# A fused RWKV-7 recurrence and MLP: chunks of 64 steps and 64x64 blocks on the quarters of the TensorE array

## The chip, the cores and the metric

The kernel runs on one NeuronCore of a Trainium2 chip, in one launch. The metric is the device time of that launch in microseconds (us), as a median over several runs. All arithmetic is float32. "Clock" is the mean clock that the throttle granted to TensorE, as a share of full speed; "half clock" is time at which it granted 0.5. In this program TensorE does the matrix products (PE in the profiles; PEld are its weight loads), and its results land in tiles of the memory called PSUM. VectorE (DVE), ScalarE (ACT) and GpSimd (POOL) copy and work on them, and SyncE (SP) issues the DMAs.

## The reference

Two blocks follow each other. The first is a recurrence over 768 steps for 4 batch entries and 8 heads of 40 channels. The second is an MLP over the 4 x 768 = 3072 tokens that come out of it.

```python
# r, k, v, w, a, b: (batch 4, heads 8, steps 768, channels 40)
for t in range(S):
    y[:, :, t] = einsum('bhd,bhde->bhe', r_t, state)
    Sa = einsum('bhde,bhe->bhd', state, a_t)
    state = state * w_t[:, :, None, :] - einsum('bhd,bhe->bhde', Sa, b_t) \
            + einsum('bhd,bhe->bhde', v_t, k_t)
x = y.transpose(0, 2, 1, 3).reshape(3072, 320)
h = x @ w_in                                  # w_in:  320 x 2048, given as float64
g = h * (1.0 / (1.0 + np.exp(-1.702 * h)))
out = g @ w_out                               # w_out: 2048 x 320, given as float64
```

## The kernel before

A chunk of C steps is computed at once. With F the product of the decays from the middle of the chunk, the kernel needs scaled inputs (kh, bh, ah), triangular C x C matrices A, N, RV and M for each head, the solution of a triangular system, and a state Z that goes from chunk to chunk:

```
A = tril(ah kh^T, -1),  N = tril(ah bh^T, -1),  SA = (I - N)^-1 (A v + ah Z^T)
(I - N)^-1 = (I + N)(I + N^2)(I + N^4) ...        (one "level" a factor)
Z' = Z + v^T kh + SA^T bh,   y = F (r Z + tril(r v^T) kh + tril(r SA^T) bh)
```

Before, a chunk has 128 steps, and a *unit* is one chunk of one batch entry with its 8 heads; there are 24 units. Heads come in pairs on the 128 partitions. The solve has seven levels.

```python
C = 128; LEVELS = C.bit_length() - 1                        # 7
ps_misc  = tile_pool(name="ps_misc",  bufs=3, space=PSUM)   # single banks of PSUM
ps_solve = tile_pool(name="ps_solve", bufs=3, space=PSUM)
ps_mlp   = tile_pool(name="ps_mlp",   bufs=2, space=PSUM)

def score(dst, lhsT, rhs, low=False):         # A, N, NT, RV, M: 64 rows, 128 columns of the array
    ps = [quad(psum(ps_misc)) for _ in range(2)]
    for q in range(NP):
        for e in range(2):
            p = slice(e * DP, (e + 1) * DP)
            mm(ps[e][:, q, :], lhsT[p, q, :], rhs[p, q, :], q == 0)
    ...                                       # masks
def level(n, e):                              # 128 x 128 products
    NT, N = s["NT"][e], s["N"][e]
    for q in range(NP):
        mm(dx[:, q], NT[:, q], xs[e][:, q], q == 0)          # 40 columns
    ...
        mm(ps[:, q], N[:, q], NT[:, q], q == 0)              # N^2, and the same for NT
# MLP of two finished units: 16 steps of `up`, 8 of `down`
for kt, (o, n) in enumerate(KT):              # 320 channels = 128 + 128 + 64
    nc.tensor.matmul(ph, w_in_sb[:n, kt, f*128:(f+1)*128], xTs[j][:n, kt, :], ...)
for f in range(part * NF // 4, (part + 1) * NF // 4):
    nc.tensor.matmul(po[u], gTs[j][f][:, u*C:(u+1)*C], w_out_sb[:, f, :], ...)
```

The main loop gives each engine its instructions in a fixed order. `weave(main, side)` issues the steps of unit i's solve and spreads two things through them: the preparation of unit i+1, and MLP steps of finished units (or, in the first units, the conversion of the float64 weights). The loads of unit i+2 are issued after the last step of unit i.

```python
for i, (c, b) in enumerate(units):
    ...
    weave(solve(i), mixed(side, mlp))
    load(i + 2)
```

Of the kernel before, what the change touches and what calls it, by code (L numbers as in the profile page):

```python
# [1 line left out]

# [19 lines left out]

# The recurrence, for one head and a chunk of C = 128 steps, with F_t the product of the decays
# from the middle of the chunk up to t (exclusive; its inverse before the middle), per key channel:
#
#   S_t = Z_t diag(F_t),  kh = k / F_{t+1},  bh = -b / F_{t+1},  ah = a F_t
#   A = tril(ah kh^T, -1),  N = tril(ah bh^T, -1)
#   SA = (I - N)^-1 (A v + ah Z_0^T)
#   Z_C = Z_0 + v^T kh + SA^T bh
#   y  = F (r Z_0 + tril(r v^T, -1) kh + tril(r SA^T, -1) bh)  # L30
#
# The decays are positive, so F is the exponential of a sum of logarithms, which a product with a
# constant triangle takes; the middle as its origin keeps F and 1 / F small over the chunk.
# N is nilpotent, so (I - N)^-1 = (I + N)(I + N^2)(I + N^4) ... (I + N^64) exactly.
# Two heads share the 128 partitions of a channel-major tile, 64 apiece, the rest zeros.


def weave(main, side):
    """Issue main in order, with side spread evenly through it."""
    done = 0  # L40
    for i, f in enumerate(main):
        f()
        upto = len(side) * (i + 1) // len(main)
        while done < upto:
            side[done]()
            done += 1
# [3 lines left out]
def rwkv7_gelu_quick(ctx: ExitStack, tc: tile.TileContext, rT_d, k_d, v_d, w_d, a_d, b_d, w_in, w_out, out):  # L50
    nc = tc.nc
    B, S, H, D = k_d.shape
    DM = H * D
    C = 128
    MID = C // 2
    NCH = S // C
    NP = H // 2
    DP = 64
    DFF = w_in.shape[1]
    NF = DFF // 128  # L60
    KT = [(o, min(128, DM - o)) for o in range(0, DM, 128)]
    NK = len(KT)
    PIECE = max(256, DM)
    LEVELS = C.bit_length() - 1
    assert S % C == 0 and H % 2 == 0 and B % 2 == 0 and D <= DP and DFF % 128 == 0 and DM <= 512

# [3 lines left out]
    ps_misc = ctx.enter_context(tc.tile_pool(name="ps_misc", bufs=3, space=bass.MemoryType.PSUM))  # L70
    ps_solve = ctx.enter_context(tc.tile_pool(name="ps_solve", bufs=3, space=bass.MemoryType.PSUM))
    ps_mlp = ctx.enter_context(tc.tile_pool(name="ps_mlp", bufs=2, space=bass.MemoryType.PSUM))
# [4 lines left out]
    def psum(pool):  # L77
        return pool.tile([128, 512], FP32, tag="bank", name="bank")

    quad = lambda t: t.rearrange("p (q t) -> p q t", q=NP)  # L80
    heads = lambda t: t[:, :DM].rearrange("p (h d) -> p h d", h=H)
    halfheads = lambda t: t[:, :NP * D].rearrange("p (q d) -> p q d", q=NP)

    def mm(o, lhsT, rhs, start):
        nc.tensor.matmul(o, lhsT, rhs, start=start, stop=True, skip_group_check=True)  # L85

# [1 line left out]
    ident = single("ident", [128, 128])  # L88
    make_identity(nc, ident)
    upper = single("upper", [128, 128])  # L90
    nc.gpsimd.memset(upper, 1.0)
    nc.gpsimd.affine_select(out=upper, in_=upper, compare_op=ALU.is_gt, fill=0.0, base=0,
                            pattern=[[1, 128]], channel_multiplier=-1)
    lower = single("lower", [128, 128])
    nc.gpsimd.memset(lower, 1.0)
    nc.gpsimd.affine_select(out=lower, in_=lower, compare_op=ALU.is_gt, fill=0.0, base=0,
                            pattern=[[-1, 128]], channel_multiplier=1)
    # [u, t]: 1 where u <= t, less 1 where u is before the middle
    cums = single("cums", [128, 128])
    nc.gpsimd.memset(cums, 1.0)  # L100
    nc.gpsimd.affine_select(out=cums, in_=cums, compare_op=ALU.is_ge, fill=0.0, base=0,
                            pattern=[[1, 128]], channel_multiplier=-1)
    nc.vector.tensor_scalar_add(cums[:MID], cums[:MID], -1.0)
    halves = single("halves", [128, 2])
    nc.vector.memset(halves[:, 0:1], 1.0)
    nc.vector.memset(halves[:, 1:2], 0.0)
    nc.vector.memset(halves[MID:, 0:1], 0.0)
    nc.vector.memset(halves[MID:, 1:2], 1.0)

    upper4 = upper.unsqueeze(1).to_broadcast([128, NP, 128])  # L110
    lower4 = lower.unsqueeze(1).to_broadcast([128, NP, 128])

# [1 line left out]
    nat = [single(f"nat{i}", [128, 4, H, DP]) for i in range(2)]  # L114
    rT = [single(f"rT{i}", [128, NP, 128]) for i in range(3)]
    sn = [single(f"sn{i}", [128, H, DP]) for i in range(2)]
    z0 = [single(f"z0{i}", [128, NP, 2, DP]) for i in range(2)]
    wch = [[single(f"wch{b}{i}", [128, 2, NP, 2]) for i in range(2)] for b in range(B)]
    wz = [single(f"wz{b}", [128, NP, 2]) for b in range(B)]
    zraw = [single(f"zraw{b}", [128, NP, 2, D]) for b in range(B)]  # L120
    for t in rT:
        nc.vector.memset(t, 0.0)
    for b in range(B):
        for t in wch[b]:
            nc.vector.memset(t, 0.0)
    for t in nat:
        nc.gpsimd.memset(t[:, :, :, D:], 0.0)
    for t in sn:
        nc.gpsimd.memset(t[:, :, D:], 0.0)
    for t in z0:  # L130
        nc.gpsimd.memset(t[:, :, :, D:], 0.0)

    w_in_sb = single("w_in_sb", [128, NK, DFF])
    w_out_sb = single("w_out_sb", [128, NF, DM])

# [1 line left out]
    def load_weight(dst, src):  # L137
        P, n = dst.shape
        raw = work.tile([128, PIECE], INT64, tag="raw", name="raw")
        nc.sync.dma_start(raw[:P, :n], src)  # L140
        word = lambda dt: raw[:P, :n].bitcast(dt).rearrange("p (n two) -> p n two", two=2)
        lo, hi = word(UINT32)[:, :, 0], word(INT32)[:, :, 1]
        scale = work.tile([128, PIECE], INT32, tag="scale", name="scale", bufs=1)[:P, :n]
        frac = work.tile([128, PIECE], INT32, tag="frac", name="frac", bufs=1)[:P, :n]
        # 2 ** exponent with the sign: 0 below the range of float32, infinite above
        nc.vector.tensor_scalar(scale, hi, 20, 0x7FF, ALU.logical_shift_right, ALU.bitwise_and)  # L146
        nc.gpsimd.tensor_scalar(scale, scale, 896.0, 0.0, ALU.subtract, ALU.max)  # L147
        nc.gpsimd.tensor_scalar(scale, scale, 255.0, 2.0 ** 23, ALU.min, ALU.mult)  # L148
        nc.vector.scalar_tensor_tensor(scale, in0=hi, scalar=-2 ** 31, in1=scale,  # L149
                                       op0=ALU.bitwise_and, op1=ALU.bitwise_or)  # L150
        # the significand, in units of 2 ** -20
        nc.vector.tensor_scalar(frac, hi, 0xFFFFF, 0x100000, ALU.bitwise_and, ALU.bitwise_or)  # L152
        nc.vector.scalar_tensor_tensor(dst, in0=lo, scalar=2.0 ** -32, in1=frac, op0=ALU.mult, op1=ALU.add)  # L153
        nc.vector.scalar_tensor_tensor(dst, in0=dst, scalar=2.0 ** -20, in1=scale.bitcast(FP32),
                                       op0=ALU.mult, op1=ALU.mult)

    def load_weights():
        pieces = [(w_in_sb[:n, kt, f:f + 256], w_in[o:o + n, f:f + 256])
                  for f in range(0, DFF, 256) for kt, (o, n) in enumerate(KT)]
        pieces += [(w_out_sb[:, f, :], w_out[f * 128:(f + 1) * 128, :]) for f in range(NF)]  # L160
        return [lambda d=d, s=s: load_weight(d, s) for d, s in pieces]

    units = [(c, b) for c in range(NCH) for b in range(B)]
    ins, ws, Fs, Gs, st = {}, {}, {}, {}, {}

# [1 line left out]
    def load(i):  # L167
        c, b = units[i]
        ts = slice(c * C, (c + 1) * C)
        got = {}  # L170
        for n, d in (("k", k_d), ("b", b_d), ("a", a_d), ("v", v_d)):
            got[n] = work.tile([128, H, D], FP32, tag="in_" + n, name="in_" + n)
            nc.sync.dma_start(got[n], d[b, ts])
        for e in range(2):
            nc.sync.dma_start(rT[i % 3][e * DP:e * DP + D, :, :],
                              rT_d[b].rearrange("(q e) d s -> e d q s", e=2)[e][:, :, ts])
        ins[i] = got

    def load_w(i):
        c, b = units[i]  # L180
        ws[i] = work.tile([128, DM], FP32, tag="in_w", name="in_w", bufs=B)
        nc.sync.dma_start(ws[i], w_d[b, c * C:(c + 1) * C].rearrange("t h d -> t (h d)"))

# [1 line left out]
    def decay(i):  # L185
        c, b = units[i]
        if b == 0:
            nc.scalar.preload_act_table_set("natural_log_exp_and_others")
# [210 lines left out]
    for b in range(B):  # L399
        load_w(b)  # L400
# [45 lines left out]
```

## Time and profile before

| | before |
|---|---|
| median of 3 runs | 2014.02 us (2001.07 to 2020.12) |
| profiled span | 1992.4 us |
| TensorE busy | 94% |
| VectorE, ScalarE, GpSimd busy | 32%, 22%, 10% |

Three lines of the page of the kernel before, beside those that the prediction quotes: the granted clock in 40 equal slices in tenths (9 is 90% or more), the engines' shares of the chain of work that ended last, and one of the costliest groups. A group's row has the line, the engine, the operation, its output and inputs, sizes, the count, then busy us and mean ns of one, then the idle time of the engine just before.

```profile
PEclk9758688998999999889999899999999998999999
...
PE 87%; DVE 6%; POOL 4%; issue 2%; ACT 1%; ACTq 0%; POOLq 0%; DVEq 0%
...
L85 PE MATMUL bank<-xs,NT 128*128 128x40 f32 x2688 | 360.4, 285 | 17.6 <-DVE xs L286 10.3
```

TensorE makes 87% of the chain that sets the end, so only its work and its waits matter. The largest single group multiplies a 128x128 block by just 40 columns: it is the costliest for the work that it does. After the weights the clock is at 0.8 or more.

### The profile page before, as it was taken

To read this page: it belongs to the slowest core of one execution; us is meant where nothing else is said; L and a number is where in the kernel's file an instruction comes from. 1 tells how busy PE (TensorE), PEld (TensorE's weight loads), DVE (VectorE), ACT (ScalarE), POOL (GpSimd) and SP (SyncE) were. 2 spreads that over 40 slices of the span, in tenths; PEclk is the share of its full clock that TensorE was granted. 3 is DMA by queue.
4 is the path that set the end of the run, shared out by engine and by line. 5 is a ranking of instruction groups with operands and counts; after the bars stand their busy time and mean duration, and the time that the engine had idled before them with its cause. 6 is when DMAs were issued, how large, how long until landed. Compare 5 with 4: busy or idle time off the path is not lost.

```text
span 1992.4 us, 31126 instructions
## 1 busy us (share of the span) xinstructions
PE 1863.5 (94%) x13608; PEld 1604.9 (81%) x13608; DVE 630.5 (32%) x1380; ACT 435.0 (22%) x872; POOL 206.4 (10%) x266
## 2 busy tenths in 40 slices
PE   6756599999999999999999999999999999999999
PEld 5756587887988888888788888788788788898885
DVE  4444432232223323223323223323323332323221
ACT  2101022222112322112322112322222222212211
POOL 3454510000000000000000000000000000000000
PEclk9758688998999999889999899999999998999999
DMA  2121200010010010010001001001001001000000
GB/s 81 46 68 39 81 8 1 5 50 1 4 37 1 1 54 1 1 40 1 1 20 35 1 5 37 1 5 50 1 4 37 1 4 37 1 4 21 1 4 11
DMA packets 34281, 40.02 MB, mean 20 GB/s; under 512 B 3424, under 2 KB 29536, under 8 KB 34144
## 3 DMA queue, kind: packets, MB, share of 16 engines
q1 hardware_dynamic: 34144, 38.02, 6.2%
q8 instruction: 107, 1.75, 0.4%
q14 instruction: 30, 0.25, 0.0%
HBM read 34.08 MB, written 3.93 MB: 19 GB/s over the span
## 4 chain that ended last, share of the span: by engine, by line
PE 87%; DVE 6%; POOL 4%; issue 2%; ACT 1%; ACTq 0%; POOLq 0%; DVEq 0%
PE bank L85 57%; PE bank L368 15%; PE bank L384 11%; PE bank L226 3%; POOL scale L148 2%; POOL scale L147 2%; DVE scale L149 1%; DVE M L216 1%; DVE frac L152 1%; DVE w_in_sb L153 0%; DVE scale L146 0%; ACT logw L190 0%; DVE w_out_sb L153 0%; DVE N L309 0%; DVE xT L351 0%
## 5 line engine op out<-in xcount | busy, mean ns | idle before, releaser
L85 PEld LDWEIGHTS bank<-xs,NT 128*128 128x128 f32 x2688 | 343.2, 198 | 66.7 <-issue 41.8
L85 PE MATMUL bank<-xs,NT 128*128 128x40 f32 x2688 | 360.4, 285 | 17.6 <-DVE xs L286 10.3
L85 PE MATMUL bank<-NT,N 128*128 128x128 f32 x2304 | 342.7, 294 | 31.7 <-DVE xs L302 31.6
L368 PE MATMUL bank<-xT,w_in_sb 128*128 128x256 f32 (+1 forms) x1152 | 334.7, 414 | 0.0
L85 PEld LDWEIGHTS bank<-NT,N 128*128 128x128 f32 x2304 | 293.8, 200 | 33.2 <-DVE xs L302 32.9
L298 ACT COPY NT<-bank 128x512 f32<-128x512 f32 x288 | 168.8, 586 | 672.8 <-PE bank L85 672.8
L309 DVE COPY N<-bank 128x512 f32<-128x512 f32 x240 | 165.8, 691 | 341.0 <-PE bank L85 340.9
L368 PEld LDWEIGHTS bank<-xT,w_in_sb 128*128 128x128 f32 (+1 forms) x1152 | 194.1, 195 | 90.7 <-issue 77.6
L85 PE MATMUL bank<-N,NT 128*128 128x128 f32 x1920 | 266.3, 284 | 0.0
L85 PEld LDWEIGHTS bank<-N,NT 128*128 128x128 f32 x1920 | 246.7, 201 | 0.0
L384 PE MATMUL bank<-w_out_sb,g 128*128 128x320 f32 x768 | 227.8, 442 | 0.0
L384 PEld LDWEIGHTS bank<-w_out_sb,g 128*128 128x128 f32 x768 | 141.7, 194 | 48.9 <-issue 3.1
L373 DVE TENSOR_TENSOR g<-bank,sg 128x256 f32<-128x256 f32 x192 | 81.5, 425 | 300.6 <-ACT sg L371 300.6
L371 ACT ACTIVATE sg<-bank 128x256 f32<-128x256 f32 x192 | 73.7, 384 | 364.1 <-PE bank L368 364.1
L302 DVE TENSOR_TENSOR xs<-xs,bank 128x160 f32<-128x160 f32 x288 | 91.8, 319 | 161.0 <-PE bank L85 157.4
L219 POOL TENSOR_SCALAR_AFFINE_SELECT RV<-RV 128x512 f32<-128x512 f32 x24 | 15.6, 650 | 762.9 <-ACT RV L217 762.9
L226 PE MATMUL bank<-ident,nat 128*128 128x128 f32 x384 | 60.9, 284 | 0.2 <-DVE RV L216 0.2
L85 PE MATMUL bank<-nat,RV 128*128 128x40 f32 x384 | 50.9, 295 | 8.1 <-DVE M L216 8.1
L147 POOL TENSOR_SCALAR scale<-scale 128x256 int32<-128x256 int32 (+2 forms) x40 | 46.4, 1160 | 109.2 <-DVE scale L146 109.2
L85 PEld LDWEIGHTS bank<-nat,RV 128*128 128x128 f32 x384 | 48.1, 203 | 11.6 <-DVE M L216 8.7
L85 PE MATMUL bank<-nat,M 128*128 128x40 f32 x384 | 56.6, 315 | 0.0
L219 POOL TENSOR_SCALAR_AFFINE_SELECT A<-A 128x512 f32<-128x512 f32 x24 | 15.9, 663 | 382.2 <-DVE A L216 296.5
(102 smaller groups left out, 1453.6 us busy)
## 6 DMA issues: line engine op xcount, KB each, us to landing
raw<-in_w_out SPq DMA_DIRECT2D x16, 320.0 KB
raw<-in_w_in SPq DMA_DIRECT2D x16, 256.0 KB
in_w<-in_w SPq DMA_DIRECT2D x24, 160.0 KB
in_k<-in_k SPq DMA_DIRECT2D x24, 160.0 KB
in_b<-in_b SPq DMA_DIRECT2D x24, 160.0 KB
in_a<-in_a SPq DMA_DIRECT2D x24, 160.0 KB
in_v<-in_v SPq DMA_DIRECT2D x24, 160.0 KB
rT<-in_rT SPq DMA_DIRECT2D x48, 80.0 KB
```

The source lines that it names most:

```text
L85: nc.tensor.matmul(o, lhsT, rhs, start=start, stop=True, skip_group_check=True)
L147: nc.gpsimd.tensor_scalar(scale, scale, 896.0, 0.0, ALU.subtract, ALU.max)
L148: nc.gpsimd.tensor_scalar(scale, scale, 255.0, 2.0 ** 23, ALU.min, ALU.mult)
L219: nc.gpsimd.affine_select(out=dst[1], in_=dst[1], compare_op=ALU.is_gt, fill=0.0, base=0, pattern=[[0, NP], [s, 128]], channel_multiplier=-s)
L226: nc.tensor.transpose(ps[:, q, :], src(q), ident)
L298: nc.scalar.copy(s["NT"][e], ps)
L302: nc.vector.tensor_add(new, xs[e], dx)
L309: nc.vector.tensor_copy(s["N"][e], ps)
L368: nc.tensor.matmul(ph, w_in_sb[:n, kt, f * 128:(f + 1) * 128], xTs[j][:n, kt, :], start=kt == 0, stop=kt == NK - 1)
L371: nc.scalar.activation(sg, ph, ACT.Sigmoid, scale=1.702)
L373: nc.vector.tensor_mul(g, ph, sg)
L384: nc.tensor.matmul(po[u], gTs[j][f][:, u * C:(u + 1) * C], w_out_sb[:, f, :], start=f == 0, stop=f == NF - 1)
```

## The change

The chunk goes to 64 steps, so that each triangle is one 64x64 block. A unit is now one chunk of two batch entries, 16 heads; there are still 24 units. Every product becomes a set of 64x64 blocks, which the profile shows as tiles of 64*64. Here a quarter of the array is named by the partition half of a block's inputs (its row half) and that of its output (its column half). The list `QUARTERS` walks round the four, so that four products in a row use four different quarters (a few products of the decays use two). The host lays the inputs out in that order. A level needs one tile W = [N | x | NT], and the solve has six. PSUM is used in pairs of banks, a bank for each row half, and the four pairs are divided so: one for the miscellaneous products, two for the levels, one for the MLP. In the diff, cuts are marked by "..." and some remarks after # are added.

```diff
-    C = 128
+    C = 64
 ...
+    LEVELS = 6
+    LAG = 2
+    HALF = [slice(0, 64), slice(64, 128)]
+    QUARTERS = [(0, 0), (1, 1), (0, 1), (1, 0)]
 ...
-    ps_misc = ctx.enter_context(tc.tile_pool(name="ps_misc", bufs=3, space=bass.MemoryType.PSUM))
-    ps_solve = ctx.enter_context(tc.tile_pool(name="ps_solve", bufs=3, space=bass.MemoryType.PSUM))
-    ps_mlp = ctx.enter_context(tc.tile_pool(name="ps_mlp", bufs=2, space=bass.MemoryType.PSUM))
+    ps_misc = ctx.enter_context(tc.tile_pool(name="ps_misc", bufs=1, space=bass.MemoryType.PSUM))
+    ps_solve = ctx.enter_context(tc.tile_pool(name="ps_solve", bufs=2, space=bass.MemoryType.PSUM))
+    ps_mlp = ctx.enter_context(tc.tile_pool(name="ps_mlp", bufs=1, space=bass.MemoryType.PSUM))
 ...
-        return pool.tile([128, 512], FP32, tag="bank", name="bank")
+        return pool.tile([128, 2, 512], FP32, tag="pair", name=name)
 ...
+        def level(n, b):
+            w = W[b]
+            ps = psum(ps_solve, "ps_level")
+            lo, hi = (0 if n < LEVELS - 2 else 64), (168 if n < LEVELS - 1 else 104)
+            for j in BITS:
+                o = j * 168
+                for h, t in QUARTERS:
+                    mm(ps[HALF[t], h, o + lo:o + 104], w[HALF[h], t, j, 104:], w[HALF[h], t, j, lo:104], j == 0)
+                if hi == 168:
+                    for h, t in QUARTERS:
+                        mm(ps[HALF[t], h, o + 104:o + 168], w[HALF[h], t, j, :64], w[HALF[h], t, j, 104:], False)
 ... x is carried along by a product with the identity; one copy of 672 columns ends the level
+            copy = nc.scalar.copy if b else nc.vector.tensor_copy
 ...
+        def score_RV():            # the other misc products (A, N, Av, zT, ahZ, saT, Z, M, rz, y, xT) alike
+            ps = psum(ps_misc, "ps_RV")
+            for e, b in product(BITS, BITS):
+                for f, u in QUARTERS:
+                    o, j = (2 * e + b) * 64, 4 * u + 2 * e + b
+                    mm(ps[HALF[u], f, o:o + 64], vT[HALF[f], j], s["rT"][HALF[f], j], o == 0)
 ...
+            nc.gpsimd.tensor_mul(x[HALF[0]], y[HALF[0]], F[HALF[0]])     # was one VectorE product
 ...
-            ph = psum(ps_mlp)[:, :2 * C]
-            for kt, (o, n) in enumerate(KT):
-                nc.tensor.matmul(ph, w_in_sb[:n, kt, f * 128:(f + 1) * 128], xTs[j][:n, kt, :], ...
+            ph = psum(ps_mlp, "ps_up")
+            for k in range(NK):
+                for r, h in QUARTERS:
+                    nc.tensor.matmul(ph[HALF[h], r, :256], w_in_sb[HALF[r], k, m, h * 64:(h + 1) * 64],
+                                     xTs[j][HALF[r], k, :], start=k == 0, stop=k == NK - 1)
 ...
             for f in range(part * NF // 4, (part + 1) * NF // 4):
-                nc.tensor.matmul(po[u], gTs[j][f][:, u * C:(u + 1) * C], w_out_sb[:, f, :], ...
+                for r, b in QUARTERS:
+                    o = p * 128 + b * 64
+                    nc.tensor.matmul(po[p][HALF[b], r, :DM], gTs[j][f // 2][HALF[r], f % 2, o:o + 64],
+                                     w_out_sb[HALF[r], f, :], start=f == 0, stop=f == NF - 1)
             if part == 3:
-                nc.scalar.copy(ob, po.pop(u))
+                nc.scalar.copy(ob, two[:, 0, :DM])
+                nc.vector.tensor_add(ob, ob, two[:, 1, :DM])       # adds the two row halves
 ... weights spread over the first four units instead of two; MLP two groups behind (LAG)
```

## The prediction

> **What bounds the kernel now.** I read the page first: its busy row, its slices and its costliest groups.
>
> ```profile
> PE 1863.5 (94%) x13608; PEld 1604.9 (81%) x13608; DVE 630.5 (32%) x1380; ACT 435.0 (22%) x872; POOL 206.4 (10%) x266
> ...
> PE   6756599999999999999999999999999999999999
> ```
>
> TensorE is busy everywhere but in the first five or six slices (about 257 us), where the weights are converted; no other engine reaches a third. But "busy" says nothing of how full the array is, so the next question is what one matmul costs. The timeline of 1000 to 1012 us:
>
> ```profile
> 999.94 0.97 PEld L85 LDWEIGHTS bank<-NT,N 128*128 128x128 f32 x8
> ...
> 1000.83 0.97 PEld L85 LDWEIGHTS bank<-N,NT 128*128 128x128 f32 x8
> ...
> 1001.73 0.97 PEld L85 LDWEIGHTS bank<-xs,NT 128*128 128x128 f32 x8
> 1001.84 0.98 PE L85 MATMUL bank<-xs,NT 128*128 128x40 f32 x8
> ...
> 1007.52 1.92 PEld L384 LDWEIGHTS bank<-w_out_sb,g 128*128 128x128 f32 x8
> 1007.63 2.32 PE L384 MATMUL bank<-w_out_sb,g 128*128 128x320 f32 x8
> ```
>
> Four matmuls of the program are eight rows: each fp32 product is two passes, each with its own weight load. Eight loads start every 0.89 us, 111 ns a pass, whether the moving side is 128 or 40 columns: the load of 128 columns sets the pace and a 40-column product is paid as a 128-column one. A pass of 320 columns takes (2.32 - 0.44) / 7 = 268 ns, so about 0.82 ns a column from 128 up. Two more rows, from 1025 and 1609 us, show what small tiles do:
>
> ```profile
> 1025.22 0.97 PEld L85 LDWEIGHTS bank<-aT,kT 64*128 64x128 f32 x16 [0.17 <-issue]
> ```
>
> ```profile
> 1608.81 0.39 PEld L85 LDWEIGHTS bank<-halves,logw 128*40 128x40 f32 x16 [0.44 <-issue]
> 1608.81 0.47 PE L85 MATMUL bank<-halves,logw 128*40 128x2 f32 x16
> ```
>
> The first alternates the two halves of the rows: 16 passes in the time of 8, so two row tiles run at once, at the full rate. The second alternates two column halves: 16 loads of 40 columns at (390 - 123) / 15 = 18 ns each, 36 ns for a round of two. So two column tiles load at once as well. Nothing in this trace uses four quarters at once.
>
> [...]
>
> **The change on TensorE.** The order of instructions per engine gives 7120 products before and 16208 after, so 32416 passes instead of 14240. All after are 64x64 blocks, issued round the four quarters. If four run at once, a round of four costs what one pass costs now, with 64 columns to load: between 36 ns (40 columns) and 111 (128) that is 57 ns; with 104 moving columns 91, with 80 71, with 256 216, with 320 268 (0.82 ns a column from 111 at 128). Rounds = products x 2 / 4:
> - recurrence, transposes and reads of up to 64 columns: 9536 products, 4768 rounds x 57 = 272 us;
> - the solve's fused products of 104 columns: 768 x 91 = 70; its identity products that carry x along: 576 x 71 = 41;
> - decays: 192 x 36 + 48 x 137 + 48 x 268 (two quarters only) = 27;
> - MLP up: 960 x 216 = 207; down: 768 x 268 = 206.
>
> Sum 823 us. The same bookkeeping for the kernel before gives 9968 x 111 + 1920 x 56 + 384 x 18 + 1152 x 216 + 768 x 268 + 48 x 268 = 1688, against 1863 busy. So the MLP hardly gains (down 206 before and after; up some 250 and its mode changes to 207); the gain is the recurrence, about 1230 to 410: chunks of 64 halve the area of each triangular product, a level fewer in the solve, and blocks fit 40 channels better. At the granted clock of 0.96 seen from 250 us on, 823 becomes 857.
>
> **The other engines.** With 0.16 + 1.04 ns an element from the VectorE rows (160: 319, 512: 691 ns) its new 672-element copies cost 0.86 us, ScalarE's 0.71 (512: 586). Per unit VectorE then has about 11.8 us of recurrence and 3.3 of MLP, ScalarE 13.4 with its table loads, GpSimd about 5. Times 24, plus 76 us of weights: VectorE 440, ScalarE 320, GpSimd 200. None bounds; TensorE has 857 / 24 = 36 us a unit.
>
> **What TensorE waits for.** The pools shrink: misc products had three banks in turn, and now one pair, so each misc product waits until the one before is copied out: some 0.2 us from the last pass to the copy, the copy (0.43 to 0.85)[...]. There are 17 a unit. Where a solve level (0.75 us) or an MLP step (2.18 us) stands between, this is hidden. I walked the order of a steady unit: the levels of the two halves alternate with side work, and wait for nothing. Its end reads N, saT, MLP step, Z, Av, M, MLP step, rz, y, MLP step, xT, zT, ahZ, level: there I find N' 0.8, saT 1.2, Av 0.8, M 0.8, y 0.8, xT 0.6 (behind two VectorE and GpSimd steps), zT 1.2, ahZ 0.8, first level 0.6, and 0.9 of scraps before: 8.5 us; odd units have the decays, about 2 more. So 9.5 a unit, for the 20 units that carry MLP: 190 us.
>
> Start: 22 us as now. Weights: they now spread over four units with their GpSimd and VectorE parts pipelined, but these units have no MLP beside them: VectorE 12 + 19 us of work each in order with waits, so about 38 a unit, 150 us in place of the 68 of TensorE counted above: +82. End: the last two MLP groups run alone with one PSUM pair, and each of 16 up steps waits for sigmoid (0.59) and product (0.69), about 1.5 us: +28 with the last output.
>
> Sum: 857 + 190 + 82 + 22 + 28 = 1179 us of span; runs are 1.1% over the span (2014 to 1992), and I add 30 us for queueing on VectorE and ScalarE: **1220 us**.
>
> **The rivals.**
> 1. Issue binds. 32416 passes and as many loads in 823 us is 12.7 ns an instruction. The fastest seen is 16 pairs in 0.39 us, 12 ns, in a burst.[...] For: nothing in the trace excludes it. Against: the bursts that it has show no trace of it. One in ten.
> 2. Quarters that share rows or columns disturb each other (two moving streams and two loads from one row half, two writers to one column half). If rounds cost 1.4 times: 823 becomes 1150, and part of the waits is covered, about 1480. One in five.
> 3. PSUM and the chain bind harder: if the waits are 15 us a unit, about 1330; if the weave hides more, 1080.
> 4. Instruction fetch or clock: doubled instruction bytes at half the time, four times the 1.75 MB's rate; and a TensorE with gaps loses clock (0.52 to 0.83 in the weight slices). Some per cent each.
>
> **Range and chances.** The centre follows from the sum; 3 moves it by 130 either way, 2 sets the upper end. Predicted 1220 us, range 1040 to 1500. Faster by over 2%: 0.91; within 2%: 0.03; slower: 0.06, nearly all of it rival 1.
>
> **What will show it.** TensorE busy share should fall to 75 to 85%, with idle time before saT, Av, M, y, zT and ahZ ended by ScalarE and VectorE copies. Rounds of 64-column passes should come at 57 ns for four, up steps at 2.2 us. The last 98 us should be MLP alone, the first 170 us without it. Wrong if rounds take 80 ns or more everywhere without a named releaser (rival 2)[...], or if another engine passes 60% busy.

Some passages are cut from it, and the cuts are marked: a paragraph of background and the size of rival 1, which rest on nothing that a trace or run of this case shows, and one part of the cost of a wait, the way back from the end of a copy to the next product. The sum came to 857 + 190 + 82 + 22 + 28 = 1179 us, and with 1.1% and 30 us to 1220. The 190 us of waits were counted with the part that is cut; in the changed kernel it is 0.06 us (the copy of M ends at 722.44 us, Av starts at 722.50). That all four quarters run at once was the assumption, carried over from two row tiles and two column tiles. The "mode changes" of the up product are the 66.1 us that PEld sat idle before its 64-row loads, which the trace puts down to "issue" and so to no cause that it shows.

## The result

The changed kernel gives the right output in 1350.03 us, median of 4 runs (1342.79 to 1351.33), against 2013.57 us (4 runs) for the kernel before. The ratio is 0.672 [0.668, 0.677]. Here and below a ratio comes from the fast runs of the two kernels alone, so it is not quite the ratio of the medians.

The page of the changed kernel:

```profile
PE 1030.6 (76%) x32416; PEld 822.6 (61%) x32416; DVE 425.2 (32%) x823; ACT 313.9 (23%) x594; POOL 214.1 (16%) x238
...
PE   4666658787787887887887887877878878878677
...
PEclk9886677898997997998899898989989989899999
...
PE 64%; DVE 13%; ACT 8%; issue 7%; DMA 5%; POOL 3%; SPq 1%; POOLq 0%; DVEq 0%; ACTq 0%
...
L512 PE MATMUL ps_up<-xT,w_in_sb 64*64 64x256 f32 x3840 | 250.0, 403 | 23.0 <-DVE g L517 20.2
L530 PE MATMUL ps_down<-w_out_sb,g 64*64 64x320 f32 x3072 | 255.0, 472 | 5.4 <-DVE g L517 2.9
```

TensorE falls from 1863 to 1031 us busy and no other engine passes a third of the span. But the slices are now at 7 and 8 tenths instead of a row of nines, the granted clock goes down to 7 and 8 tenths in many of them, and TensorE makes only 64% of the chain. The rest is copies (DVE, ACT), a DMA and issue (time in which an engine waited for nothing that the profile shows). Two windows, with PE, PEld, DVE, ACT and POOL busy us and counts, then granted clock, DMA share and GB/s, show the slow start and the steady part:

```profile
153.00:207.00 54.00, 31.59 (x1121) 27.93 (x1121) 33.44 (x72) 12.51 (x26) 34.78 (x27) 0.69 0.30 93
```

```profile
319.00:1160.00 841.00, 673.12 (x21807) 543.22 (x21803) 233.89 (x416) 212.11 (x400) 77.37 (x96) 0.91 0.11 35
```

The steady part has 16 units of 52.6 us: 42.1 busy and 10.5 idle. The waits of TensorE in it, with total us, times and the longest:

```profile
PE ps_RV L94 <- DMA in_chan<-in_chan: 28.7, 8, 4.5
PE ps_cum L94 <- ACT logw L228: 18.6, 16, 1.2
PE ps_saT L94 <- DVE W L318: 15.4, 16, 1.0
PE ps_xT L94 <- POOL x L480: 13.5, 8, 2.0
...
PE ps_ahZ L94 <- ACT zT L358: 8.7, 16, 0.5
...
PE ps_zT L94 <- DVE xT L493: 8.1, 8, 1.6
```

Most waits are short. Those of saT, ahZ and zT end with the copy of the misc product before; that of cum ends with its own input, the logarithms, and that of xT with the product y F on GpSimd. The first row is different. It is long, it comes only every second unit, and a DMA ends it. The end of an odd unit and the start of the next, in the timeline (start, us, engine, line, operation, output and inputs, count, and in brackets the idle time before it and what ended that):

```profile
714.97 0.69 PE L94 MATMUL ps_saT<-ident,sa 64*64 64x64 f32 x32 [0.97 <-DVE W L318]
...
715.46 2.36 PE L530 MATMUL ps_down<-w_out_sb,g 64*64 64x320 f32 x32
...
719.34 0.69 PE L94 MATMUL ps_N<-bhT,ahT 64*64 64x64 f32 x32 [0.60 <-DVE zraw L435]
...
721.00 0.69 PE L94 MATMUL ps_M<-in_chan,saT 64*64 64x64 f32 x32 [0.97 <-DVE W L318]
...
722.50 0.68 PE L94 MATMUL ps_Av<-in_time,A 64*64 64x40 f32 x32 [0.80 <-DVE M L447]
...
723.72 1.09 PE L94 MATMUL ps_rz<-zT,in_chan 64*64 64x40 f32 x32 [0.55 <-ACT Av L342]
...
724.60 3.56 PE L530 MATMUL ps_down<-w_out_sb,g 64*64 64x320 f32 x32
...
735.78 1.10 SPq L539 DMA_DIRECT2D out<-ob  x2
...
737.57 0.43 SPq L216 DMA_DIRECT2D in_chan<-in_chan  x1
...
744.41 1.13 PE L94 MATMUL ps_RV<-in_chan 64*64 64x64 f32 x32 [3.71 <-DMA in_chan<-in_chan]
```

Three things are to be seen. **First**, four misc products in a row (N, M, Av, rz) each wait 0.55 to 0.97 us. **Second**, the same down step takes 2.36 us at 715 and 3.56 us at 724. **Third**, SyncE's queue issues the load of `in_chan` at 737.57, right behind two stores of an output, and the product that needs it waits 3.71 us. The granted clock in windows around them, with the same columns as above:

```profile
715.00:723.60 8.60, 5.80 (x224) 4.61 (x224) 1.94 (x4) 0.94 (x2) 0.00 (x0) 1.00 0.02 4
723.60:727.00 3.40, 3.28 (x52) 2.13 (x56) 0.00 (x0) 0.49 (x2) 0.00 (x0) 0.50 0.03 7
...
744.40:747.80 3.40, 3.38 (x88) 3.04 (x92) 1.01 (x2) 0.59 (x1) 1.48 (x2) 0.54 0.02 6
```

So after a stretch in which TensorE was idle for 2.8 of 8.6 us, none of the waits over 1 us, it ran at half clock for 3.4 us (0.50 from 723.6 to 727.0); and again after the DMA wait of 3.71 us (0.54 from 744.4 to 747.8). From 319 to 1160 us there are 150 us of half clock, 9.4 us a unit. (The expectations below say 9.2; 16 units from 261 us on have as much.)

SyncE's own queue says why the load is late (us, times, longest):

```profile
SPq L539 <- DVE ob L536: 703.7, 23, 40.4
```

The issue of an output store waits for the tile `ob`, up to 40 us at a time, and a load listed behind it waits with it: in the timeline above, that of `in_chan` was issued at 737.57, after the stores that started at 735.78.

### The profile page after: what moved, and what is told of

Its sections match the earlier page's. It is cut to its first block, busy times and chain, and to the rows that moved or that the text cites. A ratio compares the mean times of both kernels' runs of the same rounds, so it can differ in the third digit from the quotient of the medians.

```text
span 1348.7 us, 67403 instructions
## 1 busy us (share of the span) xinstructions
PE 1030.6 (76%) x32416; PEld 822.6 (61%) x32416; DVE 425.2 (32%) x823; ACT 313.9 (23%) x594; POOL 214.1 (16%) x238
## 4 chain that ended last, share of the span: by engine, by line
PE 64%; DVE 13%; ACT 8%; issue 7%; DMA 5%; POOL 3%; SPq 1%; POOLq 0%; DVEq 0%; ACTq 0%
PE ps_down L530 17%; PE ps_up L512 16%; PE ps_level L94 11%; DMA in_chan<-in_chan 4%; PE ps_cum L94 3%; DVE W L318 3%; ACT sg L515 3%; PE ps_turn L94 2%; PE ps_N L94 2%; DVE g L517 2%; PE ps_y L94 2%; PE ps_saT L94 2%; PE ps_Av L94 1%; PE ps_RV L94 1%; PE ps_Z L94 1%
## 5 line engine op out<-in xcount | busy, mean ns | idle before, releaser
L512 PE MATMUL ps_up<-xT,w_in_sb 64*64 64x256 f32 x3840 | 250.0, 403 | 23.0 <-DVE g L517 20.2
L530 PE MATMUL ps_down<-w_out_sb,g 64*64 64x320 f32 x3072 | 255.0, 472 | 5.4 <-DVE g L517 2.9
L94 PE MATMUL ps_level<-W 64*64 64x64 f32 (+2 forms) x8448 | 227.5, 243 | 21.3 <-issue 10.9
L94 PEld LDWEIGHTS ps_level<-W 64*64 64x64 f32 x8448 | 209.9, 143 | 39.8 <-issue 13.1
L512 PEld LDWEIGHTS ps_up<-xT,w_in_sb 64*64 64x64 f32 x3840 | 160.9, 145 | 81.0 <-DVE g L517 26.6
L530 PEld LDWEIGHTS ps_down<-w_out_sb,g 64*64 64x64 f32 x3072 | 141.6, 149 | 76.5 <-issue 17.4
L408 DVE COPY W<-ps_level 128x672 f32<-128x672 f32 (+1 forms) x120 | 96.0, 800 | 78.2 <-PE ps_level L94 77.8
L94 PE MATMUL ps_level<-W,ident 64*64 64x80 f32 x2304 | 107.5, 242 | 2.7 <-issue 2.5
L408 ACT COPY W<-ps_level 128x672 f32<-128x672 f32 (+1 forms) x120 | 81.3, 677 | 121.2 <-PE ps_level L94 117.8
L171 POOL TENSOR_SCALAR scale<-scale 128x256 int32<-128x256 int32 (+1 forms) x36 | 47.3, 1315 | 66.1 <-DVE scale L170 65.9
L172 POOL TENSOR_SCALAR scale<-scale 128x256 int32<-128x256 int32 (+1 forms) x36 | 47.8, 1329 | 3.0
```

The lines of the kernel that those rows point to most:

```text
L94: nc.tensor.matmul(o, lhsT, rhs, start=start, stop=True, skip_group_check=True)
L171: nc.gpsimd.tensor_scalar(scale, scale, 896.0, 0.0, ALU.subtract, ALU.max)
L172: nc.gpsimd.tensor_scalar(scale, scale, 255.0, 2.0 ** 23, ALU.min, ALU.mult)
L408: copy(W[b][:, :, :, lo:], view[:, :, :, lo:])
L512: nc.tensor.matmul(ph[HALF[h], r, :256], w_in_sb[HALF[r], k, m, h * 64:(h + 1) * 64], xTs[j][HALF[r], k, :], start=k == 0, stop=k == NK - 1)
L530: nc.tensor.matmul(po[p][HALF[b], r, :DM], gTs[j][f // 2][HALF[r], f % 2, o:o + 64], w_out_sb[HALF[r], f, :], start=f == 0, stop=f == NF - 1)
```

## The experiments

Twelve kernels ran, each timed beside the kernel before on the same chip, and all give the right output. Times are medians over all runs; of serial_all two of four runs and of best_b one of four were slow. The percentages against the changed kernel are quotients of ratios. The theory was: the quarters do run at once at the predicted rates, because the products go round them; what the prediction missed is the late load, more waiting at the end of a unit, and the half clock that follows short waits. The rivals were: quarters that share rows or columns disturb each other; the MLP's form costs or gains something of its own; and the clock alone explains the difference.

### What the quarters are worth

**down_serial** changes the order of the same products in the down step.

```diff
-            for f in range(part * NF // 4, (part + 1) * NF // 4):
-                for r, b in QUARTERS:
+            for r, b in QUARTERS:
+                for f in range(part * NF // 4, (part + 1) * NF // 4):
```

> The changed kernel with the down product's four blocks of each step issued quarter by quarter (all four f of one quarter, then the next) instead of round the quarters; the same products and the same sums. If the quarters run at once only when consecutive instructions go to different quarters[...], a down step takes up to 4 x 2.15 = 8.6 us, 12 x 8 steps x 6.4 = +620 us at most: 1700 to 1970. [...]a step stays near 2.2 to 3 us: 1350 to 1430.

The condition cut from its last case is that the quarters work at once whatever the order of issue.

It took 1687.45 us, ratio 0.844 [0.838, 0.850], so 26% longer than the changed kernel. The group of its page:

```profile
L530 PE MATMUL ps_down<-w_out_sb,g 64*64 64x320 f32 x3072 | 607.4, 479 | 5.0 <-DVE g L517 2.9
```

One product takes 479 ns, as before (472). But the group is busy for 607 us instead of 255: the products overlap much less. At full clock passes of one step now start 156 ns apart on average, where they did 64 ns apart; where one quarter works alone, its passes start 269 ns apart. The 352 us more account for the whole loss of 337.

**serial_all** does the same to all products: a step's products are held back and issued sorted by quarter.

```diff
+        # the products of one step, quarter by quarter
+        quarter = lambda c: (c[0][1].start_partition(), c[0][0].start_partition())
+        for a, k in sorted(held, key=quarter):
+            tc.nc.tensor.matmul(*a, **k)
```

> The changed kernel with the same 16208 products, but within each step (each stretch of products between two copies) sorted quarter by quarter instead of round the quarters. If the gain of the change is the quarters running at once, and that hangs on the order of issue as the run with the serial down product showed (a step took 4.5 us for 2.0, two quarters at a time at most), TensorE's 823 us become about 1750 and the whole 2100 to 2400, slower than the kernel before. If the gain is the smaller chunk and the smaller blocks themselves, it stays under 1700.

It took 3360.31 us, ratio 1.662 [1.647, 1.677]: slower than the kernel before by two thirds, and far over the 2100 to 2400 that were forecast. The profile fell on a run that is 1.6% above this kernel's fastest and is so called slow. The clock of its fast runs is the same, 0.69 to 0.71. Its page, a part of its timeline at full clock with the same step of the changed kernel below it, and three windows:

```profile
PE 3155.6 (94%) x32416; PEld 2423.8 (72%) x32416; DVE 427.6 (13%) x823; ACT 316.4 (9%) x594; POOL 214.2 (6%) x238
...
PEclk9965555768776767776777776777885785856656
```

```profile
1501.33 5.51 PE L67 MATMUL ps_up<-xT,w_in_sb 64*64 64x256 f32 x36
```

```profile
776.14 2.34 PE L512 MATMUL ps_up<-xT,w_in_sb 64*64 64x256 f32 x40
```

```profile
100.00:200.00 100.00, 90.38 (x1068) 85.38 (x1069) 30.11 (x74) 12.24 (x25) 28.36 (x26) 1.00 0.14 42
...
400.00:500.00 100.00, 93.72 (x858) 79.63 (x855) 16.15 (x31) 8.27 (x13) 11.20 (x11) 0.50 0.05 17
...
2400.00:2500.00 100.00, 93.53 (x1181) 73.97 (x1179) 13.28 (x23) 9.68 (x17) 5.70 (x7) 0.83 0.07 21
```

36 passes of an up step take 5.51 us from the first start to the last end; less the last one's own 0.38 (the row of a single pass in the same view), that is 147 ns apiece. In the changed kernel a step of 40 takes 2.34 us, so 50 ns. The quarters are worth a factor of 2.9 there, and for the 64-column products 2.8 (42.5 against 15.4 ns between starts, medians over full steps of 32 passes). These are means: inside this step, where one quarter works alone, its passes start 216 ns apart, as those of the full array do, and where one quarter gives way to the next, two overlap. So the whole gain hangs on the order of issue. How much of it is the shorter chunk and how much the quarters is not set apart by any run; without the overlap all of it is lost. The forecast of 1750 us of products was too low: the clock of 0.706 loses about 990 of the 3362 us, which leaves about 2170 at full clock, and the lost clock was not forecast at all. The last fence shows something beside the question: TensorE is busy for 90 to 94 of 100 us in all three windows, and is granted 1.00, 0.50 and 0.83. So being busy did not by itself keep the clock up here. What decides is not shown, since the order of the quarters is the same in all three.

**order** changes who follows whom: quarters that share the row half now come next to each other.

```diff
-    QUARTERS = [(0, 0), (1, 1), (0, 1), (1, 0)]
+    QUARTERS = [(0, 0), (0, 1), (1, 0), (1, 1)]
```

> The changed kernel going round the quarters as (0,0), (0,1), (1,0), (1,1), so that two neighbours in issue share the row half, instead of changing the row half each time. If each quarter has its own stream and only a repeat of the same quarter blocks: no change, within 1% of 1345. If neighbours that share rows disturb each other (one row half read by two streams, the second rival of the prediction): rounds of 70 ns or more in place of 57, over 1400.

It took 1346.36 us, ratio 0.675 [0.670, 0.680], the same as the changed kernel. Its down group:

```profile
L530 PE MATMUL ps_down<-w_out_sb,g 64*64 64x320 f32 x3072 | 258.2, 477 | 5.2 <-DVE g L517 2.9
```

258 against 255 us: between these two orders it doesn't matter which quarter follows which; in both, all four take turns.

**mlp128** puts the MLP alone back to larger blocks: down as 128x128, up as two 64x128 row tiles.

```diff
-                for r, h in QUARTERS:
-                    nc.tensor.matmul(ph[HALF[h], r, :256], w_in_sb[HALF[r], k, m, h * 64:(h + 1) * 64],
+                for r in BITS:
+                    nc.tensor.matmul(ph[:, r, :256], w_in_sb[HALF[r], k, m, :],
 ...
-                for r, b in QUARTERS:
-                    o = p * 128 + b * 64
-                    nc.tensor.matmul(po[p][HALF[b], r, :DM], gTs[j][f // 2][HALF[r], f % 2, o:o + 64], ...
-                nc.vector.tensor_add(ob, ob, two[:, 1, :DM])
+                o = p * 128
+                nc.tensor.matmul(po[p][:, 0, :DM], gTs[j][f // 2][:, f % 2, o:o + 128], ...
```

> The changed kernel with the MLP not in quarters: the down product as 128x128 blocks, the up product as two 64x128 row tiles; the recurrence stays in quarters. Prediction's account: the four quarters at once move as much as the full array (8 rounds of 268 ns a down step, 10 of 216 an up step either way), so the MLP steps keep their 2.15 us, and the change of tile mode around each of 192 steps costs 0.1 to 0.3 us: 1350 plus 20 to 60, about 1385. Rival (the quartered MLP is a real part of the gain): over 1450. Other rival (fewer instructions help): under 1340.

It took 1375.82 us, ratio 0.688 [0.683, 0.694], 2.4% longer than the changed kernel. A down step in its timeline:

```profile
808.56 2.42 PE L529 MATMUL ps_down<-w_out_sb,g 128*128 128x320 f32 x8
```

Eight passes of the whole array take 2.42 us, where 32 passes on quarters take 2.35. So the MLP gains next to nothing from its new form, and nearly all of the gain is the recurrence. The 26 us more are 0.14 us for each of the 192 steps of the MLP, where the array changes its form. The traces have more. At full clock and without a wait, the time from the last pass before a down step to the first after it is 2.51 us instead of 2.19, and for an up step 2.52 instead of 2.21 (medians), and about 0.24 us of that lies at the two ends of the step. That would be some 60 us for 192 steps, so about half of it must have been hidden in waits; no run takes that apart.

### Where the time went

**early_load** issues the loads of unit i+2 as soon as their buffers are free, right after the state's update, and so ahead of the output stores of the unit's last MLP step.

```diff
-                + [back] + ([update] if i + 2 < NU else []) + [scores]
+                + [back] + ([update, lambda: load(i + 2)] if i + 2 < NU else []) + [scores]
 ...
-        if i + 2 < NU:
-            load(i + 2)
```

> The changed kernel, with the load of the unit after next issued right after the state update of a unit instead of after its last step, so that it no longer stands behind the output stores in SyncE's queue. Theory A (a load that queues behind the output stores, missed in the prediction): the 8 waits of ps_RV for in_chan (28.7 us between 319 and 1160 us) and the half-clock stretches after them go, 2.5 to 3.5 us a unit, 50 to 70 us in all: about 1290 us, ratio to the kernel before 0.64. Theory B (the wait is hidden time that other waits take over, because the unit is bound by its misc products): less than 15 us gained, 1335 to 1350.

It took 1304.33 us, ratio 0.651 [0.646, 0.656]: 3.1% less than the changed kernel. Of its waits in 319 to 1090 us, the first row is now

```profile
PE ps_cum L94 <- ACT logw L228: 17.4, 16, 1.2
```

and no row of a DMA is left among the costly ones. In a window of 16 units,

```profile
319.00:1118.00 799.00, 655.30 (x21759) 534.93 (x21752) 228.77 (x416) 208.97 (x399) 74.10 (x95) 0.92 0.12 37
```

half clock falls from 9.4 to 7.7 us a unit. Counted from one start of ps_ahZ to the next, even units, which had the wait, go from 50.9 to 46.2 us; odd ones stay at 54. The gain of 3.1%, 42 us, is less than the 50 to 70 that were expected. One reservation: the load is one more entry of the list that is woven, and so shifts some steps against each other.

**tail_mlp** leaves the loads, and in odd units puts seven of the eight down steps after the last seven steps of the unit (the last level, saT, Z, M, rz, y, xT), with the preparation of the next unit ahead of them.

```diff
+        if p and j >= 0 and len(main) == 19:
+            slots = [[] for _ in main]
+            for n, f in enumerate(side):
+                slots[1 + n * 12 // len(side)].append(f)
+            for n, f in zip((0, 12, 13, 14, 15, 16, 17, 18), mlp):
+                slots[n].append(f)
```

> The changed kernel; in units that carry the down product (odd units from the fifth on), the eight MLP steps stand between the misc products of the unit's end instead of evenly over it; nothing else moves. Theory A (one PSUM pair for all misc products: where two follow each other TensorE waits for the copy in between): the waits before N, M, Av, rz, y, zT and ahZ in odd units fall from some 13 us to 6, gain 4 to 7 us in each of 10 units, 40 to 70 us: about 1295. Theory B (these waits are data dependences of the solve, or move into the levels): within 15 us of 1350.

It took 1302.21 us, ratio 0.650 [0.645, 0.655]: 3.3% less. Counted as above, odd units went from 54.4 to 47.7 us (even ones from 50.9 to 51.5), and half clock to 4.3 us a unit. The clock of 16 units is 0.96, and the DMA wait stays, as it should:

```profile
319.00:1112.00 793.00, 638.37 (x21828) 524.20 (x21824) 232.53 (x416) 211.94 (x400) 76.45 (x97) 0.96 0.12 37
```

```profile
PE ps_RV L94 <- DMA in_chan<-in_chan: 28.5, 7, 4.7
```

**early_tail** should have joined the two, and failed as an experiment. Early load had made the list one entry longer, so that the test on 19 steps never held; what ran was early_load again.

> The changed kernel with both edits that gained: the early load and the down steps between the misc products of the end of odd units. Independent causes: the gains of 41 and 43 us add up, about 1262 us, ratio to the kernel before 0.63. If both removed the same waits, about 1300.

It took 1302.63 us, ratio 0.648 [0.644, 0.653], and so only repeats early_load. **early_tail2** hangs the load onto the update itself, which keeps the list at 19 steps and removes the reservation about the weave.

```diff
+                + [back] + ([lambda: (update(), load(i + 2))] if i + 2 < NU else []) + [scores]
 ... and the slots of tail_mlp
```

> Both edits again, now truly together: in the run before this, the early load added an entry to the list of steps and the test for 19 steps kept the old order, so that it was a second run of the early load alone. Here the load hangs on the update step itself and the order of the other steps stays. If the two gains are independent (41 and 43 us), about 1262 us, ratio 0.63. If one hides the other, about 1300, 0.65.

It took 1241.64 us, ratio 0.623 [0.617, 0.629], 7.3% less than the changed kernel. The two changes gave 0.021 and 0.022 of the ratio apart and 0.049 together: within the intervals, their sum. Its clock in slices, and the steady window:

```profile
PEclk9876765989999999999999999999999999999999
```

```profile
319.00:1048.00 729.00, 605.61 (x21417) 503.94 (x21408) 222.01 (x407) 206.43 (x394) 71.02 (x91) 0.99 0.12 40
```

The clock is 0.99 where it was 0.91, half clock is down to 1.3 us a unit, and a unit takes 46.4 us instead of 52.6. The prediction's own terms give 45.2 (823 / 24 / 0.96 of products and 9.5 of waits), so the two edits remove 6.2 of the 7.4 us of difference in a steady unit. They do not restore it term by term: TensorE is now busy for 38.6 us a unit where the prediction has 35.7, and idle for 7.8 where it has 9.5.

**fill** takes the clock alone. In odd units it issues products that nothing reads, into columns that the open down tile leaves free, ahead of the misc products that wait. The waits should stay, with TensorE just not idle in them.

```diff
+    def fill(rounds):
+        for o in filler:
+            for n in range(rounds):
+                for r, b in QUARTERS:
+                    mm(o[HALF[b], r, 384:448], ident[HALF[r]], upper[HALF[r]], False)
```

> The changed kernel; in units with the down product, TensorE gets extra products that nothing reads before each misc product that waits (in free columns of the open down tile), 0.35 to 1.4 us each, a little shorter than the wait. Waits stay the same. Theory (a stretch with many waits lowers the granted clock, so that waits are paid a second time): half-clock time falls from 9.2 us a unit to below 6, and the whole gains 10 to 25 us in spite of 7 us more TensorE work per odd unit: about 1330. Rival (the clock falls for another reason[...]): half-clock time stays or grows and the time is 1350 to 1370.

It took 1346.94 us in 5 rounds, ratio 0.671 [0.668, 0.675], the same as the changed kernel. The steady window:

```profile
319.00:1160.00 841.00, 691.80 (x24384) 572.03 (x24384) 234.27 (x416) 212.63 (x401) 77.57 (x96) 0.95 0.11 36
```

The clock rose from 0.91 to 0.95, and half clock fell from 9.4 to 5.5 us a unit, as the theory had it and the rival had not. So part of the half clock at least comes from idle time. But a unit takes 52.5 us, as before (52.6). Less what half clock loses, TensorE is busy for 40.4 us instead of 37.4: the filler costs 3.0 us a unit, and 1.9 of better clock and 1.2 of less idle time pay for it. The expected gain of 10 to 25 us did not come. Whether the clock could be had for less than the filler costs stays open.

**misc2** gives the misc products two pairs of PSUM banks and the levels one.

```diff
-    ps_misc = ... bufs=1      ps_solve = ... bufs=2
+    ps_misc = ... bufs=2      ps_solve = ... bufs=1
```

> The changed kernel with two PSUM pairs for the misc products and one for the solve's levels, in place of one and two. Theory A (one pair for misc costs the waits at the end of a unit): the waits before saT, N, M, Av, rz, y, ahZ shrink by some 6 us a unit, but now each level waits for the copy of the one before (about 1.2 us from its end) where only a misc product stands between, some 5 us a unit: 1320 to 1380, with the waits moved from the misc products to ps_level. Theory B (the waits at the end are true dependences): they stay and the levels' come on top, over 1430.

It took 1290.11 us, ratio 0.643 [0.640, 0.647], 4.3% less than the changed kernel and less than either theory expected. Its waits in 319 to 1090 us:

```profile
PE ps_level L94 <- DVE W L408: 61.2, 43, 7.6
...
PE ps_level L94 <- ACT W L408: 15.8, 30, 0.8
```

The levels now wait, about 5 us a unit. But most waits of the misc products are gone, and so is that for `in_chan`; the clock is 0.95. Why the load is in time here isn't settled: SyncE still waits for `ob`, but each unit's order of events has moved.

### A version that beats both

**best_a** joins misc2 and the early load, and moves two single steps: the product y F from GpSimd to VectorE, and the logarithms of the decays one step of the side work ahead of their first use. **best_b** joins early_tail2 with the same two steps.

```diff
-            nc.gpsimd.tensor_mul(x[HALF[0]], y[HALF[0]], F[HALF[0]])
+            nc.vector.tensor_mul(x[HALF[0]], y[HALF[0]], F[HALF[0]])
 ...
+            side += [lambda: (logs(i + 1), logs(i + 2))] + [lambda n=n: decay(i + 1 + n) for n in range(2)]
```

> Two PSUM pairs for misc and one for the levels, with the early load, the products of y and the decays on VectorE instead of GpSimd, and the logarithms of the decays one side step ahead of the products that need them. From 1290 for the two pairs alone: the xT wait of 1.35 us a unit should fall to 0.6, the cum wait of 1.19 to near 0, 45 us in all; the early load adds little since that run shows no wait for in_chan: about 1245, ratio 0.62. Rival (the level waits of 6 us a unit take over what is freed): over 1275.

> One pair for misc as in the changed kernel, with the early load, the down steps between the misc products of odd units' ends, y times decays on VectorE and the logarithms ahead. If causes add: 1262 less 24 units x 2 us = about 1215, ratio 0.605. If waits are exchanged for one another: 1240 to 1290.

best_a took 1200.83 us, ratio 0.603 [0.598, 0.608], the fastest kernel here: 10% less than the changed kernel. best_b took 1213.45 us, ratio 0.607 [0.601, 0.613]; the intervals overlap, so that best_a is not shown to be the faster of the two. (best_b's profiled run was a slow one.) best_a's page:

```profile
PE 946.9 (79%) x32416; PEld 751.5 (63%) x32416; DVE 441.1 (37%) x895; ACT 311.6 (26%) x594; POOL 167.1 (14%) x166
...
PEclk9987787999998998998999999998999999999999
```

The same 32416 products are busy for 947 us instead of 1031, which fits a clock that holds (0.954 over the span, 0.896 in the changed kernel) and fewer products that end in a wait. What each of the joined changes gives here is not set apart.

## Why the prediction was right, and where its sum was off

The direction, the order of size and the range held: 1350 us lies in 1040 to 1500. The centre of 1220 was 10% too low, and the sum under it more than that.

1. **Rates: right.** At full clock four passes of 64 columns start in 58 ns (predicted 57), a round of down takes 269 to 273 ns (268), a round of up 216 to 221 (216), and a level 0.73 to 0.75 us (0.75). The rounds of 160 columns in the decays are off, 187 ns for 137, but that is 2.4 us in all. Rival 1, that issue binds, is refuted: 823 us for 32416 passes ask for 25.4 ns each, a stretch of 192 passes with as many loads ran at 15.5 ns a pass, and all 32416 passes together took 1031 us, 32 ns each. Rival 2, quarters that disturb each other, is refuted by the rates and by the order experiment. What the prediction took for granted, "issued round the four quarters", is the condition of it all: down_serial and serial_all show it.
2. **The MLP hardly gains, the recurrence does: right.** mlp128 shows it, and its longer steps (0.14 us each over the 192) lie in the 0.1 to 0.3 us that were expected of it. Why a change of form costs time is not shown.
3. **No other engine becomes the bound, and TensorE is busy 75 to 85%: right.** It is 76%, and VectorE, ScalarE and GpSimd are busy for 425, 314 and 214 us (predicted 440, 320 and 200). Idle time before saT, M, Av, y, zT and ahZ is ended by the engines that copy, 15.4, 12.2, 13.7, 4.7, 8.1 and 8.7 us of it from 319 to 1160 us.
4. **The wait for the load: missed.** The sum has no term for a transfer. Loads behind output stores cost 1.8 us of waiting a unit, and half clock after it. early_load puts the term at 3.1%, or some 42 us; the shift of the weave is in that figure, but early_tail2 has the gain without the shift. The row of SyncE's queue is what should have been asked for: whether a load stands behind something in its queue that is late.
5. **"So 9.5 a unit": too small.** Idle time is 10.5 us a unit. To this come about 3 us that count as busy (42.1, less 4.7 for half clock, less the 34.3 that 823 / 24 gives). Rounds that are up to 2% slower and the ends of the last products before each wait would explain them; that is argued, not measured apart. So about 13.6 in place of 9.5, with 1.8 of it the late load of step 4. Rival 3 named 15 as its bad case.
6. **"At the granted clock of 0.96": too high.** That was the clock of a TensorE that hardly waited (in the kernel before it is busy for 1702 of the 1742 us from 250 us on). In the steady part it was 0.91: 9.4 us of half clock lose 4.7 us a unit, where 0.96 allowed 1.4. The prediction knew the effect as rival 4, at "some per cent". Idle time lowers it here: fill fills the waits, and early_tail2 takes waits away, and with either the half clock goes down (to 5.5 and 1.3 us).
7. **Weights: too small.** The first four units end at 207 us and not at 172. They take 42 to 54 us each instead of 38, at a clock of 0.69 to 0.86. VectorE and GpSimd are busy for 33 and 35 of the 54 us of the last of them, so neither is full. The cause was read, not tested: a chain that goes from engine to engine.
8. **End: nearly right.** The two MLP groups run alone from 1244 us on, 104 us instead of 98; an up step there waits 1.44 us (predicted 1.5).
9. **"Runs are 1.1% over the span": a wrong reading.** On every run the time is 1.7 to 2.5 us over its span, here 1350.48 to 1348.7. The 1992.4 us that the prediction compared with 2014 must then belong to a faster execution of the kernel before.

In sum: 35 us for the start, 20 units at 51.9 instead of 45.5 us for another 128, and 6 at the end take the predicted span of 1179 to 1348, and the measured one is 1348.7. The sum was short by 170 us. That the centre missed by only 130 is due to what was added to it: 30 us for queueing, and 13 from the wrong reading of step 9, which is luck. In a steady unit the 7.4 us that were missed are 1.8 of late load, 2.3 of other waits and 3.3 of half clock. The step that failed is the sum of the waits, steps 4 to 6. Its mechanism was right for the copies and its size was not: each wait was costed by itself, without the clock that is lost to it, and without the queue behind which loads stand.

## What to carry to other kernels

Small blocks on the quarters of the array paid here, where the blocks fit the problem better, and only with successive products on different quarters: round the quarters 64-column passes started 15.4 ns apart, sorted by quarter 42.5 ns, and the whole took 1350 or 3360 us. So write the loops so that the quarter is the innermost index. Once TensorE's work was that much shorter, its short waits cost time twice over: it was idle in them (10.5 us a unit) and then ran at half clock (9.4 us a unit). Long products (MLP steps) put between short ones that depend on each other took 3.3% off the time (tail_mlp), a second pair of banks for the short ones 4.3% (misc2). And look at the DMA queue by itself: here a load listed behind a store was issued after it, when the store's data was ready and not when its own buffer was free (the stores waited 703.7 us for `ob`); a product waited 3.71 us for it, and with the loads ahead of the stores the kernel took 3.1% less (early_load).
